# Attention output with d on partitions, in 64x32 array tiles and shared TensorE blocks, in a fused attention-and-MoE kernel

## The chip, the cores and the metric

One core of one Trainium2 chip. The metric is device microseconds (us) of one execution of the whole program. The kernel before takes 190.25 us, the median of three runs (190.19 to 191.84). TensorE is called PE below, VectorE DVE, ScalarE ACT, GpSimd POOL. A "pair" is one weight load and the matmul that uses it: two PE instructions.

## The reference

```python
# attention: q, k, v, alpha are (4, 8, 768, 48)
for t in range(S):
    state = alpha[:, :, t, :, None] * state + np.einsum('bhd,bhe->bhde', k[:, :, t], v[:, :, t])
    y[:, :, t] = np.einsum('bhd,bhde->bhe', q[:, :, t], state)
# MoE: x is y reordered to (3072, 384); w_in (384, 2048), w_out (2048, 384)
h = x @ w_in
r = np.maximum(h, 0.0)
return (r * r) @ w_out
```

The kernel computes the recurrence in chunks: inside a chunk by masked scores, between chunks through a state of 48 x 48 numbers per head. It works in 12 units, each of 256 time steps of one batch entry.

## The kernel before

A small list scheduler in the kernel orders all work. Each `add("pe", ...)` below is one block of PE instructions that is never split: the scheduler takes the block of highest priority whose inputs its own model says are there.

Of one unit's PE blocks these matter here (cut):

```python
def kv(pe):                                   # what a chunk adds to the state
    for p in range(NPR):
        for j in range(2):
            for ab in halves:
                ro = slice(ab * HP, (ab + 1) * HP)
                ins = pe.matmul(psY[ab][:, p * 96:p * 96 + 96],
                                QKS[qs][ro, 0, j, 2 * p:2 * p + 2, :].rearrange("p h d -> p (h d)"),
                                VBF[vb][ro, j, p * 96:p * 96 + 96], ...)
...
for hp in range(2):
    def score(pe, hp=hp, pb=pb):              # 16 matmuls in 64x64 tiles
        for i in range(2):
            p = 2 * hp + i
            for j in range(2):
                for ab in range(2):
                    for h in range(2):
                        ro = slice(64 * h, 64 * h + 64)
                        ins = pe.matmul(pb[ab * HP:(ab + 1) * HP, h, (2 * i + j) * C:(2 * i + j + 1) * C],
                                        KQT[kt][ro, 0, j, p, ab * HP:(ab + 1) * HP],
                                        KQT[kt][ro, 1, :, p, ab * HP:(ab + 1) * HP])
    add("pe", score, ...)                     # then the mask, on DVE
def y(pe):                                    # time on partitions
    ...  # 16 matmuls q x state, then 32 masked scores x v
add("pe", y, ...)
...  # two copies to XBF on ACT
def xt(pe):                                   # turns y so that d is on partitions, as the MoE wants it
    ...  # 6 transposing matmuls
add("pe", xt, ...)
...  # copy to XT on DVE
```

The MoE of a unit follows: s1 (48 matmuls of 256 columns) and s2 (32 of 384 columns), in blocks of 6 and 4. The block m1 computes running sums of log alpha.

```python
M1_FROM = 3
pa, pakey = (psTF[:], ("ps", "T")) if u >= M1_FROM else (psP[:, 0, :], ("ps", "P"))
```

## Time and profile before

| | before |
|---|---|
| time, us | 190.25 |
| span in the profile, us | 189.2 |
| PE matmuls | 2283 |
| PE busy | 94% |
| DVE / ACT / POOL busy | 59% / 69% / 46% |

From the page of the kernel before: busy time of the engines, the span in 40 slices of 4.7 us (a digit is a busy share in tenths), the queue that brings instructions, and the chain of work that ended last.

```profile
PE 178.7 (94%) x2283; PEld 125.4 (66%) x2283; DVE 112.3 (59%) x154; ACT 131.3 (69%) x253; POOL 86.8 (46%) x97
...
PE   7899899996989899999999999999999999999993
...
PEclk9999999999999999999999999999999999999999
DMA  6999999999999999981997982955315218110102
...
q8 instruction: 18, 0.29, 0.6%
...
PE 66%; DMA 15%; SPq 7%; DVE 5%; POOL 3%; issue 1%; ACT 1%; POOLq 0%; DVEq 0%
```

PE is the limit on paper: 94% busy. The DMA row: its engines are nearly full for the first 18 slices, about 85 us.

The wait view of PE (what it waited for, us in total, times, longest):

```profile
PE psY L628 <- DVE pm L615: 1.5, 1, 1.5
PE psO L387 <- DVE warm L378: 1.3, 1, 1.3
PE psH L687 <- ACT rr L696: 1.1, 2, 0.8
```

These and six smaller ones come to about 7 us. "Issue" is time in which PE waits for nothing that the profile shows.

The timeline of PE at one y (start, us, engine, line, operation, output <- inputs, weights, data, count). Durations overlap, so cost is read from start to start:

```profile
113.66 0.36 PE L628 MATMUL psY<-sbd,kqt 128*64 128x96 bf16 x8
113.86 0.34 PE L628 MATMUL psY<-sba,kqt 128*64 128x96 bf16 x8
114.12 0.57 PE L636 MATMUL psY<-vbf,pm 64*128 64x48 bf16 x32
114.63 1.48 PE L687 MATMUL psH<-xt,win 128*128 128x256 bf16 x12
```

L628 is the part of y that comes from the state, L636 that inside a chunk: y takes 0.97 us, from 113.66 to 114.63. The xt, elsewhere in the timeline, takes 0.34 and a kv 0.45.

### The profile page before, as it was taken

The numbers are of one execution on the slowest core, as the hardware profiler recorded it, in microseconds if no ns is written. First come the engines' busy times: TensorE is split into PE (matmuls) and PEld (weight loads), VectorE is DVE, ScalarE is ACT, GpSimd is POOL, SyncE is SP. The second block draws the span as 40 slices with busy tenths as digits, with TensorE's granted clock in tenths as the row PEclk, the third lists the DMA queues.
The fourth block names the chain that finished last, engine by engine and source line by source line (L and its number), as shares of the span: only waits on it lengthen the run. The fifth ranks groups of instructions, "written<-read, shape, count | busy, mean of one in ns | idle before, by whom it ended". The sixth has DMA issues, their size and how long they took to land.

```text
span 189.2 us, 5328 instructions
## 1 busy us (share of the span) xinstructions
PE 178.7 (94%) x2283; PEld 125.4 (66%) x2283; DVE 112.3 (59%) x154; ACT 131.3 (69%) x253; POOL 86.8 (46%) x97
## 2 busy tenths in 40 slices
PE   7899899996989899999999999999999999999993
PEld 2345676674566577768677767676677687677771
DVE  6788662889959449748368576267156185441230
ACT  2658799878696667858849749579567476477552
POOL 6224686635284356554735725534723354243100
PEclk9999999999999999999999999999999999999999
DMA  6999999999999999981997982955315218110102
GB/s 156 325 364 377 385 371 268 268 287 286 291 228 263 225 225 309 201 236 42 142 319 108 247 250 53 238 157 71 85 45 97 59 42 114 42 45 27 56 3 83
DMA packets 76119, 34.95 MB, mean 185 GB/s; under 512 B 69440, under 2 KB 74560, under 8 KB 76096
## 3 DMA queue, kind: packets, MB, share of 16 engines
q1 hardware_dynamic: 76096, 34.61, 71.4%
q8 instruction: 18, 0.29, 0.6%
q14 instruction: 5, 0.04, 0.1%
HBM read 25.17 MB, written 4.72 MB: 158 GB/s over the span
## 4 chain that ended last, share of the span: by engine, by line
PE 66%; DMA 15%; SPq 7%; DVE 5%; POOL 3%; issue 1%; ACT 1%; POOLq 0%; DVEq 0%
PE psH L687 28%; PE psO L717 25%; DMA raw<-in_q_dram 7%; SPq L470 6%; DMA stg<-in_moe_w_in_dram 5%; PE psP L608 4%; DMA kqt<-qks 3%; PE psY L636 2%; PE psY L628 2%; DVE pm L615 2%; DVE qks L531 2%; PE psY L573 2%; PE psTF L654 1%; PE psH L717 1%; POOL gt L703 1%
## 5 line engine op out<-in xcount | busy, mean ns | idle before, releaser
L703 POOL TENSOR_TENSOR gt<-rr 128x512 bf16<-128x512 bf16 x45 | 52.3, 1165 | 56.5 <-ACT rr L696 51.9
L687 PE MATMUL psH<-xt,win 128*128 128x256 bf16 x576 | 72.3, 273 | 1.1 <-ACT rr L696 1.1
L717 PE MATMUL psO<-wout,gt 128*128 128x384 bf16 x368 | 68.9, 326 | 1.6 <-ACT gt L700 1.1
L696 ACT ACTIVATE rr<-psH 128x512 bf16<-128x512 f32 x96 | 56.8, 598 | 10.7 <-PE psH L687 9.2
L687 PEld LDWEIGHTS psH<-xt,win 128*128 128x128 bf16 x576 | 53.9, 98 | 12.2 <-ACT rr L696 1.4
L717 PEld LDWEIGHTS psO<-wout,gt 128*128 128x128 bf16 x368 | 34.3, 98 | 21.0 <-ACT gt L700 1.2
L615 DVE TENSOR_TENSOR pm<-psP,mask 128x1024 bf16<-128x1024 f32 x23 | 28.1, 1223 | 18.9 <-PE psP L608 18.9
L703 DVE TENSOR_TENSOR gt<-rr 128x512 bf16<-128x512 bf16 x28 | 18.5, 662 | 28.2 <-ACT rr L696 28.2
L725 ACT ACTIVATE osb<-psO 128x384 f32<-128x384 f32 x23 | 11.3, 489 | 27.2 <-PE psO L717 27.0
L531 DVE TENSOR_TENSOR qks<-raw,asb 128x768 bf16<-128x768 f32 x24 | 29.2, 1250 | 1.3 <-ACT asb L519 1.3
L500 POOL TENSOR_TENSOR raw<-raw,ral 128x384 f32<-128x384 f32 x12 | 12.1, 1005 | 8.3 <-ACT ral L495 7.1
L492 ACT ACTIVATE lab<-raw 128x768 bf16<-128x768 f32 x12 | 10.1, 843 | 6.8 <-DVE raw L490 6.8
L700 ACT ACTIVATE gt<-rr 128x512 bf16<-128x512 bf16 x23 | 14.4, 627 | 0.4
L387 PE MATMUL psO<-warm 128*128 128x512 bf16 x43 | 13.4, 442 | 1.3 <-DVE warm L378 1.3
L648 ACT ACTIVATE xbf<-psY 128x384 bf16<-128x384 f32 x24 | 10.6, 493 | 3.7 <-PE psY L636 3.6
L660 DVE COPY xt<-psTF 128x768 bf16<-128x768 bf16 x12 | 6.7, 556 | 10.3 <-PE psTF L654 10.3
L593 POOL TENSOR_TENSOR sba<-tmp,acm 128x384 bf16<-128x384 f32 x8 | 6.6, 830 | 10.9 <-DVE tmp L591 10.9
L593 POOL TENSOR_TENSOR sbd<-tmp,acm 128x384 bf16<-128x384 f32 x8 | 7.3, 915 | 7.7 <-DVE tmp L591 7.7
L524 ACT ACTIVATE vbf<-rav 128x768 bf16<-128x768 f32 x12 | 10.1, 840 | 0.5 <-DMA rav<-in_v_dram 0.5
L490 DVE TENSOR_TENSOR raw<-raw 128x384 f32<-128x384 f32 x12 | 8.3, 688 | 3.1 <-DMA raw<-in_alpha_dram 3.1
L608 PE MATMUL psP<-kqt 64*64 64x128 bf16 x368 | 9.6, 222 | 0.4 <-ACT kqt L558 0.2
L608 PEld LDWEIGHTS psP<-kqt 64*64 64x64 bf16 x368 | 5.9, 106 | 5.7 <-issue 3.5
(68 smaller groups left out, 141.9 us busy)
## 6 DMA issues: line engine op xcount, KB each, us to landing
raw<-in_alpha_dram SPq DMA_DIRECT2D x12, 384.0 KB, 5.1
raw<-in_k_dram SPq DMA_DIRECT2D x12, 384.0 KB, 4.7
raw<-in_q_dram SPq DMA_DIRECT2D x12, 384.0 KB, 4.9
rav<-in_v_dram SPq DMA_DIRECT2D x12, 384.0 KB, 5.1
out_dram<-osb SPq DMA_DIRECT2D x24, 192.0 KB, 2.1
stg<-in_moe_w_in_dram SPq DMA_DIRECT2D x4, 768.0 KB, 8.0
stg<-in_moe_w_out_dram SPq DMA_DIRECT2D x4, 768.0 KB, 7.4
kqt<-qks SPq DMA_TRANSPOSE x18, 3.7
```

Source lines behind the costliest of these rows:

```text
L387: o = Op("pe", lambda pe: pe.matmul(psO[:, 0:512], WARM[:, 0:128], WARM[:], start=not begun, stop=True, skip_group_check=True), 216, 0, "w")
L470: chain("sp", lambda e, dst=dst, src=src: e.dma_start(dst, src), 400, 2 * u * P - 4 * P + o, writes=[key], name=f"ld{nm}{u}", dma=f"{nm}{v ...
L500: add("pool", lambda e: e.tensor_tensor(q0, q0, heads(RAL[0][:]), ALU.mult), 1000, pu + 520, reads=[("raw", r, 1), ("ral",)], writes=[("ra ...
L531: add("dve", lambda e, t=t: e.tensor_tensor(QKS[qs][:, t, :, :, 0:D].rearrange("p j h d -> p h j d"), RAW[r][:, t, :, :].rearrange("p h (j ...
L593: add("pool", lambda e, dst3=dst3, acm=acm, ab=ab: e.tensor_tensor(dst3, TMP[ab][:].rearrange("p (n d) -> p n d", d=D), acm, ALU.mult), 10 ...
L608: ins = pe.matmul(pb[ab * HP:(ab + 1) * HP, h, (2 * i + j) * C:(2 * i + j + 1) * C], KQT[kt][ro, 0, j, p, ab * HP:(ab + 1) * HP], KQT[kt][ ...
L615: add("dve", lambda e, pm=pm, pb=pb: e.tensor_tensor(PM[pm][:].rearrange("p h i s -> p (h i) s"), pb[:, :, :].rearrange("p h (i s) -> p (h ...
L687: ins = pe.matmul(psH[:, hb, i * n:(i + 1) * n], WIN[:, kk, fj * 128:(fj + 1) * 128], XT[:, kk, g0 * C:g0 * C + n], start=(kk == 0), stop= ...
L696: add("act", lambda e, hb=hb, rb=rb: e.activation(RR[rb][:], psH[:, hb, :], AF.Relu), act_ns(512), pu + 600, reads=[("ps", "H", hb)], writ ...
L700: add("act", lambda e, sq=sq, dst=dst: e.activation(dst, sq, AF.Square), 560, pu + 1200, reads=[("rr", rb)], writes=[("gt", gt, u)], name= ...
L703: add(how, lambda e, sq=sq, dst=dst: e.tensor_tensor(dst, sq, sq, ALU.mult), {"dve": 560, "pool": 1100}[how], pu + 1200, reads=[("rr", rb) ...
L717: ins = pe.matmul(po, GT[gt][:, fj, ti * C:(ti + 1) * C], WOUT[:, fj, :], start=(fj == 0), stop=(fj == FT - 1))
```

## The change

The intent: PE is the limit, so spend less of it per unit. y is computed with d on partitions, so xt and one of the two ACT copies go; DVE now copies half of y itself to XT (6.7 us in all, as its copy of xt took before). All attention matmuls use tiles of 64 rows x 32 columns, eight at once where before four 64x64 tiles ran. In y the program never lets the upper and the lower rows write the same PSUM bank at once: they change banks behind a semaphore (more on it under "What could not be tried"). From unit 5 on, kv and a score share one block and so do y and the next unit's score, which saves changes of tiling. States keep only their used columns. MOE_OFF moves the MoE later in the schedule.

The core of the diff (cuts marked with `...`):

```diff
+    def kv_part(u):
+        r, vr, la, a, qs, kt, vb = bufs(u)
+        halves = range(1 if is_last(u) else 2)
+
+        def fn(pe):
             for p in range(NPR):
                 for j in range(2):
-                    for ab in halves:
-                        ro = slice(ab * HP, (ab + 1) * HP)
-                        ins = pe.matmul(psY[ab][:, p * 96:p * 96 + 96],
-                                        QKS[qs][ro, 0, j, 2 * p:2 * p + 2, :].rearrange("p h d -> p (h d)"),
-                                        VBF[vb][ro, j, p * 96:p * 96 + 96], start=(p == 0 and j == 0),
-                                        stop=(j == 1), skip_group_check=True)
+                    for q4 in range(4):
+                        for ab in halves:
+                            ro = slice(ab * HP, (ab + 1) * HP)
+                            h, d0 = 2 * p + q4 // 2, 32 * (q4 % 2)
+                            ins = pe.matmul(psY[ab][32 * q4:32 * q4 + 32, p * D:(p + 1) * D],
+                                            QKS[qs][ro, 0, j, h, d0:d0 + 32], VBF[ro, vb, j, h, 16:DP],
+                                            start=(p == 0 and j == 0), stop=(j == 1), skip_group_check=True)
             return ins
...
+        return (fn, KV_NS, [("qks", qs, 0), ("vbf", vb)], [("ps", "Y", ab) for ab in halves], 2 * u * P + 2700,
+                f"kv{u}")
...
+    def score_part(u, hp):
+        kt = u % NKQT
+        pb, key = (psH, [("ps", "H", 0), ("ps", "H", 1)]) if u == 0 and hp else (psP, [("ps", "P")])
+
+        def fn(pe):
+            for i in range(2):
+                p = 2 * hp + i
+                for j in range(2):
+                    for q4 in range(4):
+                        ab = q4 // 2
+                        for h in range(2):
+                            ro = slice(64 * h, 64 * h + 64)
+                            ins = pe.matmul(pb[32 * q4:32 * q4 + 32, h, (2 * i + j) * C:(2 * i + j + 1) * C],
+                                            KQT[kt][ro, 0, j, p, 32 * q4:32 * q4 + 32],
+                                            KQT[kt][ro, 1, :, p, ab * HP:(ab + 1) * HP])
+            return ins
+
+        return fn, P_NS, [("kqt", kt, 0), ("kqt", kt, 1)], key, 2 * u * P + 3800 + 10 * hp, f"p{hp}{u}"
...
+        g0b, g1a = rounds(inter(0, 1)), [] if first else rounds(inter(1, 0))
+        g0a, g1b = ([] if first else rounds(inter(0, 0))) + rounds(intra(0)), rounds(inter(1, 1)) + rounds(intra(1))
+        if SWAP_SEM:
+            streams = (g0b + g0a, [[]] * len(g0b) + g1b) if first else (g0b + g0a, g1a + g1b)
+        elif first:
+            streams = (g0b + g0a, [[]] * 3 + g1b)
+        else:
+            streams = (g0b + [[]] * 2 + g0a, [[]] + g1a + g1b)
+
+        def fn(pe):
+            begun = set()
+            for k in range(max(len(s) for s in streams)):
+                if SWAP_SEM and k == len(g0b):
+                    turns[0] += 1
+                    ins.then_inc(turn, 1)
+                    pe.wait_ge(turn, turns[0])
+                both = [s[k] if k < len(s) else [] for s in streams]
+                for c in range(4):
+                    for part in both:
+                        if not part:
+                            continue
+                        t, ab, w, x = part[c]
+                        ins = pe.matmul(psY[ab][32 * c:32 * c + 32, (t // 4) * C:(t // 4 + 1) * C], w, x,
+                                        start=(ab, c) not in begun, stop=True, skip_group_check=True)
+                        begun.add((ab, c))
...
+    SWAP_SEM = True
...
+    def block(*parts):
+        def fn(pe):
+            for p in parts:
+                ins = p[0](pe)
...
-        p0 = 2 * m * P + 22000
+        p0 = 2 * m * P + MOE_OFF          # 30000
...
+    FUSE_FROM = 5
...
+        if w >= FUSE_FROM:
+            block(kv_part(w), score_part(w, 1))
...
+        if u < U and u >= FUSE_FROM:
+            block(y_part(w), score_part(u, 0))
+        else:
+            block(y_part(w))
+            if u < U:
+                block(score_part(u, 0))
```

The matmuls of a unit's kv go from 16 to 64, of a score from 16 to 32, of y and xt from 54 to 96 (the last and the first chunks have fewer).

## The prediction

> **What bounds it now.** TensorE. The page gives PE 94% of 189.2 us; the chain that ended last is 66% PE, from about 64 us unbroken PE work but for one evacuation at the end. The waits view gives PE only about 7 us of waits, nearly all before 64 us. Until about 80 us DMA is near its ceiling (slice row), yet PE has MoE work to fill in: it is busy with useful matmuls from 19 us on. The two MoE groups take, by the starts of instructions, 109 ns x 576 = 63 us and 162 ns x 384 = 62 us, and don't change. ACT 69%, DVE 59%, POOL 46% are not limits.
>
> So what counts is PE time per attention unit (12 units). From the starts of blocks in the timeline: m1 0.29, inter-chunk y 0.46, intra y 0.51, transpose xt 0.34, kv 0.45, two scores 0.35 each, and each change of array tiling costs: the MoE block before a tiled block is 1.42 instead of 1.31 us (0.11 in), and of the score's 350 ns only 4 x 56 are matmuls (0.126 out). In total about 3.1 us a unit.
>
> **What changes, costed.**
> - Scores become 32 instead of 16 matmuls each, in 64x32 tiles: eight tiles at once instead of four. In the trace four 64x64 tiles start within 10 ns, rounds 56 ns apart. I estimate the same 4 x 56 ns with eight tiles. [...] no trace here shows eight yet.
> - kv: 64 matmuls, 8 rounds of 48 columns. Estimate 26 to 35 ns a round, 0.21 to 0.28, plus 0.24 for the switches: saves 0.1.
> - y gives d on partitions, so xt (0.34), its DVE copy (6.7 us in all) and one of two ACT evacuations go. y is 12 rounds of 128 columns, 0.67, plus the semaphore between row groups: 216 ns of the last matmul, about 50 ns to the waiter as DVE's mask shows, a restart, less one round: about 0.24. So 1.14 with switches, against 1.37 with xt.
> - From unit 5 on kv+score and y+score share a block, each saving one switch, 0.24. [...]
> - m1 loses one 28 ns matmul.
> - State work on half the columns: DVE about 5 us, POOL about 6 us less in all; off the path.
>
> Sum: seven fused units save about 0.83 us each, five early ones 0.17 to 0.36 each (the first chunk had only half the inter-chunk work, but still needs 12 rounds). About 6.8 us, nearly all on the critical path, as PE has backlog throughout. I add nothing for DVE, ACT and POOL; MOE_OFF only moves MoE later, where it runs dense.
>
> **Prediction: 183.5 us, 8 in 10 between 180.5 and 187.5. Faster by over 2%: 0.80; within 2%: 0.16; slower: 0.04.**
>
> **What would show it right.** PE blocks: kv+score about 0.56 us from its first matmul to the next block, y+score about 1.26; rounds of eight 56 ns apart; one gap of about 0.29 us inside each y; no transposes to the xt; MoE groups still 109 and 162 ns apart; PE again without waits after 64 us; DVE near 107 us, ACT near 126.
>
> **What would make it wrong.** [...] kv rounds bound by weight loads at 56 ns: 2 to 3 us back. A semaphore gap of 0.5 us: 2.5 us back. Fused blocks waiting on the mask (1.2 us on DVE) or the transposing DMA. New PE idle in the DMA-bound first 70 us.

The sum came to about 6.8 us, and 190.25 less 6.8 is 183.5. The trace of before stands behind these estimates as far as it goes. Rounds of two matmuls of 48 columns start 25 ns apart (the inner y, 114.2 to 114.5 us), near the 26 of the kv; for the 35 the record names no source, nor for weight loads as a bound of the kv rounds. The score's last matmul is recorded as 216 ns long, the mask on DVE starts 51 ns after its end, and the first round of a score takes 80 ns and not 56 (the restart). The state work that is halved took 11.0 us on DVE and 13.9 on POOL.

## The result, and the profile after

The kernel after takes 202.06 us, the median of four runs (200.34 to 203.53; the run of 203.53 is not in the ratio). Executions over 1.5% slower than the fastest of the same kernel are left out of the means. The ratio to the kernel before is 1.056 (95%: 1.047 to 1.066): slower by 5.6%. A ratio here is the mean time of one kernel's fast runs over the mean of the other's in the same rounds, so it is not quite the ratio of the medians. The prediction, 183.5, had the wrong sign.

The same lines of the page of the kernel after (its slices are 5.0 us):

```profile
PE 179.5 (90%) x3609; PEld 123.5 (62%) x3613; DVE 104.1 (52%) x150; ACT 127.9 (64%) x241; POOL 83.3 (42%) x93
...
PE   7986598788997949977999999999999999999994
...
PEclk9999999999999996999999999999999999999999
DMA  6999999998999997999998105928143511010112
...
q8 instruction: 28, 0.46, 1.0%
...
PE 63%; DMA 13%; SPq 10%; ACT 5%; issue 5%; DVE 4%
```

PE is hardly busier in us, but it is idle more: the digits 5, 7, 4, 7, 7 all lie before slice 20. One digit of PEclk is a 6. The chain has 5% "issue". The instruction queue moves 28 packets.

The wait view of PE:

```profile
PE psY L578 <- issue: 3.0, 2, 2.7
PE psH L748 <- issue: 2.4, 2, 1.8
...
PE psP L617 <- issue: 1.3, 1, 1.3
```

The waits "for nothing" are new. The largest in the timeline:

```profile
70.70 0.60 PE L578 MATMUL psY<-vbf,qks 64*32 64x48 bf16 x56
73.97 0.22 PE L578 MATMUL psY<-vbf,qks 64*32 64x48 bf16 x8 [2.66 <-issue]
74.11 0.42 PE L617 MATMUL psP<-kqt 64*32 64x128 bf16 x32
74.46 0.87 PE L748 MATMUL psH<-xt,win 128*128 128x256 bf16 x6
75.12 2.77 PE L778 MATMUL psO<-wout,gt 128*128 128x384 bf16 x8
```

PE stops for 2.7 us after 56 of a kv's 64 matmuls. Nothing in the program stands between the 56th and the 57th: no wait, no change of tiling, no new buffer. The s2 matmuls of the last line then start 319 ns apart instead of 162: the clock record of the trace has PE at half clock from 75.1 to 78.5 us.

**Where the stops fall.** I numbered PE's own records (weight loads, matmuls and the few of its sequencer) together, in the order of their starts. There are six stops of over 0.25 us inside blocks, and all have a number that leaves 188 to 192 when divided by 256:

| stop begins, us | 16.4 | 21.1 | 46.8 | 71.1 | 93.8 | 105.8 |
|---|---|---|---|---|---|---|
| from last start to next start, us | 0.69 | 2.08 | 0.83 | 2.85 | 1.50 | 0.55 |
| inside | y | s1 | s1 | kv | score | kv |
| this page of 256 was used up in, us | 5.8 | 4.0 | 4.8 | 2.1 | 3.7 | 3.7 |

In sum 8.5 us (a stop is counted from the start of the last instruction to the start of the next, so a little more than the idle time in the views). The instruction queue brings 28 packets of 16,384 bytes for 7283 PE records, 260 to a packet; in before 18 for 4613, 256 to a packet. That PE's records stop every so often at the same place modulo 256 suggests one packet, or page, for 256 instructions. The kernel before has no such stop; there a page of PE lasts 7.1 to 12.2 us.

For the six stops, and in the last two rows for later boundaries with DMA less busy, the times of the packet that came in between (which packets belong to PE is inferred from the order):

| previous page entered, us | packet starts | packet ends | PE resumes | turnaround, us |
|---|---|---|---|---|
| 10.55 | 14.75 | 15.71 | 17.05 | 6.5 |
| 17.05 | 20.75 | 21.73 | 23.16 | 6.1 |
| 41.98 | 45.34 | 46.27 | 47.62 | 5.6 |
| 68.97 | 71.65 | 72.64 | 73.97 | 5.0 |
| 90.07 | 92.93 | 93.86 | 95.30 | 5.2 |
| 102.10 | 104.12 | 105.04 | 106.35 | 4.3 |
| 129.74 | 130.75 | 131.88 | 133.26, a stop of 0.2 | 3.5 |
| 143.36 | 144.11 | 145.04 | 146.67, no stop | under 3.3 |

In each of these rows the packet comes only after the page before its own is entered. In the six rows of the stops, where the DMA engines are full, it starts 2.0 to 4.2 us after that; in the last two rows, where the slice of the packet has a DMA digit of 2 and of 1, after 1.0 and 0.8 us. Then it takes about 1 us, and PE goes on 1.3 to 1.4 us later. I read this as a load of instructions that queues behind the data; the runs below test it. Rows chosen by their stops could mislead, so here are all page boundaries of the 18 traces of this document. Where packets of data kept the engines over 85% busy (233 boundaries), half of the instruction packets start about 2.0 us or more after the page is entered; where under 40% (144 boundaries), half start within 0.8 us. The spread is wide (in the first group from 2.0 us before to 5.0 us after), so full DMA makes a late packet likely and not certain. And in every stop of these traces PE goes on 1.1 to 1.6 us after a packet of the instruction queue has ended: it is the packet that ends the stop. A stop is what the turnaround takes beyond the time in which the page was used up: 0.7 us in the first row (6.5 less 5.8), 2.9 in the fourth (5.0 less 2.1). Over all of these traces a packet comes at most 2.3 us before the page before its own is entered (in before at most 1.3 us, at 149.1 us for a page entered at 150.4).

**What else moved.** Late in the run, with DMA light, blocks can be read undisturbed. A fused kv and score, and a fused y and score:

```profile
115.79 0.71 PE L578 MATMUL psY<-vbf,qks 64*32 64x48 bf16 x64
116.31 0.48 PE L617 MATMUL psP<-kqt 64*32 64x128 bf16 x32
116.73 0.61 PE L748 MATMUL psH<-xt,win 128*128 128x256 bf16 x4
...
128.84 0.71 PE L690 MATMUL psY<-kqt,sta 64*32 64x128 bf16 x32
129.37 0.74 PE L690 MATMUL psY<-pm,vbf 64*32 64x128 bf16 x64
129.90 0.48 PE L617 MATMUL psP<-kqt 64*32 64x128 bf16 x32
130.32 0.50 PE L748 MATMUL psH<-xt,win 128*128 128x256 bf16 x3
```

kv takes 0.53 us (116.31 less 115.79), the block 0.94. y and score take 1.48 (130.32 less 128.84). In the records of single instructions about the first 64 of such a block, 32 pairs, run at full pace (in y counted anew from its semaphore): from round to round 55 to 56 ns in y after the first, and 39, 27 and 26 in the kv of 93.24 us, whose next round comes after 128. From there on a pair starts every 8.3 ns, so a round of eight takes 67 ns and not 56. It is 8.3 ns for the 48 columns of a kv as for the 128 of a score, so the columns do not set it. I call it issue; what in PE sets it is not shown.

And the first units come late. After, at the second unit:

```profile
36.73 0.33 PE L498 MATMUL psP<-lab,lblk 128*128 128x384 bf16 x1
...
38.38 0.42 PE L617 MATMUL psP<-kqt 64*32 64x128 bf16 x32
...
40.71 0.29 PE L690 MATMUL psY<-kqt,sta 64*32 64x128 bf16 x8 [1.35 <-DVE pm L627]
```

The same score and y before:

```profile
25.36 0.42 PE L608 MATMUL psP<-kqt 64*64 64x128 bf16 x16
...
27.34 0.36 PE L628 MATMUL psY<-sba,kqt 128*64 128x96 bf16 x8
```

The y of unit 1 starts 13.4 us later. Ahead of its score now stands an m1 that writes the same psP: the m1 of unit 2, whose inputs arrive only then. Counting MoE matmuls at 109.3 and 162.5 ns each, before has done 56.3 us of MoE work by 100 us, after 45.9. The spans differ by 10.9 us; nearly all of it is there by 100 us. (Attention is behind as well, by about a unit: the y of unit 6 starts at 100.7 us in before, that of unit 5 at 101.3 in after. The gain late in the run makes up for that.)

### The profile page after: what moved, and what is told of

Its sections match the earlier page's. It is cut to its first block, busy times and chain, and to the rows that moved or that the text cites. A ratio compares the mean times of both kernels' runs of the same rounds, so it can differ in the third digit from the quotient of the medians.

```text
span 200.1 us, 7982 instructions
## 1 busy us (share of the span) xinstructions
PE 179.5 (90%) x3609; PEld 123.5 (62%) x3613; DVE 104.1 (52%) x150; ACT 127.9 (64%) x241; POOL 83.3 (42%) x93
## 4 chain that ended last, share of the span: by engine, by line
PE 63%; DMA 13%; SPq 10%; ACT 5%; issue 5%; DVE 4%
PE psH L748 25%; PE psO L778 25%; SPq L463 9%; PE psY L690 5%; DMA stg<-in_moe_w_in_dram 4%; PE psP L617 3%; DMA raw<-in_alpha_dram 3%; DMA rav<-in_v_dram 3%; DMA kqt<-qks 3%; PE psY L578 2%; DVE qks L521 2%; ACT rr L757 1%; PE psH L778 1%; ACT win L436 1%; DVE pm L627 1%
## 5 line engine op out<-in xcount | busy, mean ns | idle before, releaser
L748 PE MATMUL psH<-xt,win 128*128 128x256 bf16 x576 | 73.8, 273 | 3.1 <-issue 2.4
L764 POOL TENSOR_TENSOR gt<-rr 128x512 bf16<-128x512 bf16 x45 | 49.9, 1110 | 53.4 <-ACT rr L757 53.4
L521 DVE TENSOR_TENSOR qks<-raw,asb 128x768 bf16<-128x768 f32 x24 | 27.5, 1162 | 7.8 <-ACT asb L508 7.8
L601 POOL TENSOR_TENSOR sta<-tmp,acm 128x192 bf16<-128x192 f32 x16 | 13.0, 815 | 21.3 <-DVE tmp L599 21.2
L722 DVE CAST xt<-psY 128x384 bf16<-128x384 f32 x12 | 6.7, 557 | 17.7 <-PE psP L617 14.0
L617 PE MATMUL psP<-kqt 64*32 64x128 bf16 x736 | 11.1, 225 | 3.0 <-DMA kqt<-qks 1.3
L719 ACT ACTIVATE xt<-psY 128x384 bf16<-128x384 f32 x12 | 5.9, 490 | 10.3 <-PE psP L617 5.8
L617 PEld LDWEIGHTS psP<-kqt 64*32 64x32 bf16 x736 | 7.4, 91 | 5.8 <-issue 2.2
L578 PE MATMUL psY<-vbf,qks 64*32 64x48 bf16 x640 | 7.1, 186 | 4.2 <-issue 3.0
L690 PE MATMUL psY<-pm,vbf 64*32 64x128 bf16 x768 | 9.7, 221 | 0.8 <-issue 0.5
## 6 DMA issues: line engine op xcount, KB each, us to landing
stg<-in_moe_w_in_dram SPq DMA_DIRECT2D x4, 768.0 KB, 10.3
```

The source lines that it names most:

```text
L521: add("dve", lambda e, t=t: e.tensor_tensor(QKS[qs][:, t, :, :, 0:D].rearrange("p j h d -> p h j d"), RAW[r][:, t, :, :].rearrange("p h (j ...
L617: ins = pe.matmul(pb[32 * q4:32 * q4 + 32, h, (2 * i + j) * C:(2 * i + j + 1) * C], KQT[kt][ro, 0, j, p, 32 * q4:32 * q4 + 32], KQT[kt][ro ...
L690: ins = pe.matmul(psY[ab][32 * c:32 * c + 32, (t // 4) * C:(t // 4 + 1) * C], w, x, start=(ab, c) not in begun, stop=True, skip_group_chec ...
L748: ins = pe.matmul(psH[:, hb, i * n:(i + 1) * n], WIN[:, kk, fj * 128:(fj + 1) * 128], XT[:, kk, g0 * C:g0 * C + n], start=(kk == 0), stop= ...
L764: add(how, lambda e, sq=sq, dst=dst: e.tensor_tensor(dst, sq, sq, ALU.mult), {"dve": 560, "pool": 1100}[how], pu + 1200, reads=[("rr", rb) ...
```

## The experiments

Theories:

- **F, fetch.** Denser instructions use up a page sooner than the next can be fetched. PE stops.
- **I, issue rate.** Beyond the first 32 pairs of a block a pair costs 8.3 ns, so 32-column tiles give less than estimated.
- **Q, order.** New block order and fused blocks make the first units, and all MoE behind them, late: m1 of unit 2 ahead of the second score of unit 1; y of unit 4 in one block with a score of unit 5, for which it must wait.
- **M, MoE offset.** MOE_OFF alone delays MoE work that PE then lacks.

All results in one table. Stops are those of over 0.25 us at the same place modulo 256, inside a block, from each profile. "MoE" is the MoE work done by 100 us, as above. The ratio is to the kernel before, run on the same chip in the same session.

| run | what it is | us | ratio (95%) | stops: n, us | y of unit 1 / 4 starts | MoE |
|---|---|---|---|---|---|---|
| before | | 190.25 | 1 | 0 | 27.3 / 74.2 | 56.3 |
| after | | 202.06 | 1.056 (1.047 to 1.066) | 6, 8.5 | 40.7 / 89.1 | 45.9 |
| a_t64 | after, kv and scores in 64x64 | 194.60 | 1.013 (1.005 to 1.020) | 3, 4.4 | 38.7 / 82.7 | 49.8 |
| a_off22 | after, MOE_OFF of before | 200.42 | 1.043 (1.036 to 1.051) | 8, 8.7 | 40.1 / 80.8 | 50.9 |
| a_nofuse | after, no fused blocks | 199.92 | 1.047 (1.039 to 1.054) | 6, 8.0 | 40.7 / 78.9 | 47.0 |
| b_p32 | before, scores in 64x32 | 190.64 | 0.998 (0.991 to 1.006) | 0 | 27.6 / 74.1 | 56.5 |
| a_m2 | after, m1 from unit 2 on elsewhere | 199.32 | 1.046 (1.041 to 1.050) | 8, 9.1 | 29.6 / 86.3 | 49.6 |
| a_t64_m2 | both | 191.02 | 1.002 (0.999 to 1.005) | 2, 1.0 | 25.4 / 81.6 | 53.9 |
| a_thin | after, few late input bytes | 197.01 | 1.033 (1.025 to 1.041) | 3, 4.8 | 41.8 / 86.8 | 47.5 |
| b_thin | before, the same | 190.33 | 0.998 (0.994 to 1.002) | 0 | 27.3 / 73.5 | 56.8 |
| a_shift | after, 120 extra weight loads first | 209.27 | 1.095 (1.089 to 1.101) | 7, 11.8 | 44.8 / 92.0 | 43.3 |
| a_t64_m2_off22 | a_t64_m2, MOE_OFF of before | 194.43 | 1.020 (1.013 to 1.027) | 2, 2.0 | 25.6 / 82.3 | 51.9 |
| a_best | a_t64_m2, first score inside y | 190.95 | 1.000 (0.995 to 1.006) | 4, 4.6 | 25.5 / 81.1 | 52.2 |
| a_best22 | a_best, MOE_OFF of before | 195.11 | 1.024 (1.017 to 1.030) | 3, 2.6 | 25.2 / 81.1 | 53.5 |
| a_f7 | after, fused from unit 7 | 206.23 | 1.073 (1.066 to 1.080) | 8, 13.8 | 41.7 / 81.2 | 44.7 |
| a_t64_m2_f7 | a_t64_m2, fused from unit 7 | 190.99 | 0.994 (0.988 to 0.999) | 1, 0.8 | 25.4 / 75.8 | 55.7 |
| a_best_f7 | a_best, fused from unit 7 | 193.05 | 0.995 (0.986 to 1.004) | 3, 3.1 | 26.2 / 78.9 | 52.4 |
| a_best_f8 | a_best, fused from unit 8 | 187.95 | 0.979 (0.973 to 0.985) | 1, 1.0 | 25.5 / 75.7 | 54.2 |

All gave the reference's result but a_thin and b_thin, which are wrong. Stops, starts and MoE come from one profiled run each. The medians are of all runs, slow ones too (one each in after, a_t64 and a_off22, two in a_best_f7); the ratios are of fast runs alone. Runs come from four sessions besides that of after, and before took 190.5 to 191.7 us in them (medians). So a difference of us between sessions is good to about 1 us, and the ratios are the fairer measure. By them after loses 10.7 us to before, a_t64 is 8.3 us under after, a_off22 2.5, a_m2 2.1, a_nofuse 1.9, a_t64_m2 10.3, a_thin 4.5; a_f7 is 3.1 and a_shift 7.4 over it.

### a_t64: fewer, larger tiles for kv and scores

```diff
-                    for q4 in range(4):
+                    for q2 in range(2):
...                      # kv: 64-row and 64-column tiles, 32 matmuls for 64
-                    for q4 in range(4):
-                        ab = q4 // 2
+                    for ab in range(2):
...                      # score: 16 matmuls for 32
```

> The kernel after, with kv and score back in 64x64 tiles (same rows, same columns, half the matmuls); y stays in 64x32. Theory F (fetch): PE stops at fixed places, every 256 PE instructions, because pages of instructions are used up faster than the next one lands; 8 such stops cost about 8.5 us in the trace of after. Fewer instructions in a burst (about 5,750 PE records instead of 7,283) should leave 3 us of stops or less. Theory I (issue): beyond the first 64 instructions of a block one weight load and matmul pair takes 8.3 ns, so 64-matmul kv blocks take 0.6 us; here kv falls to 0.25 to 0.35 us and scores to 4 x 56 ns, about 3 us in all. F and I together: 191 to 194 us. Theory O (order: later MoE and fused blocks hold PE up): stays at 200 to 202 us.

Measured 194.60 us, 7.5 us under the kernel after, with 5879 PE records for 7283 and three stops of 4.4 us in all. The time lies just above the range I gave, 191 to 194, and the stops, 4.4 us, are more than the 3 I expected. The fall of 4.1 us in stops (8.5 less 4.4) is a good half of the gain; the rest I put down to the kv, bound by issue, and to the clock that no longer fell (mean granted clock of the profiled runs 1.000 for 0.991), without having parted them. In blocks late in the run: a full kv and a score take 0.60 us where after has 0.94, but y and a score take 1.56 where after has 1.48, as the tiling now changes inside that block. F and I both get support; this run does not part them.

### b_p32: the opposite, one denser block in the kernel before

```diff
-                        for ab in range(2):
+                        for q4 in range(4):
+                            ab = q4 // 2
...                          # score: 32 matmuls for 16, as in after
```

> The kernel before with only the scores in 64x32 tiles: 368+ more matmuls, as many more weight loads, in 24 separate blocks with MoE work around them. F (it is the rate in a burst, not the count): no stop at a 256 boundary, as a page still lasts 6 us or more. I: each block lasts 32 x 8.3 = 267 ns instead of 224, in all +1 us: 190.8 to 192. If instead every further page of instructions costs a stop of 1 us or so whatever the rate: 193.5 or more.

Measured 0.998: the same. The cost of I that I expected here did not come: the scores take 9.76 us in sum (from start to next start) against 9.71, so 32 pairs in a block that stands alone run at full pace. Only the two scores of unit 0, which follow each other without a break, take longer: from their first start to their last 538 ns with 64 pairs, 425 ns before with 32. It shows that eight tiles at once are no problem by themselves, and no stops appear when only the scores get denser. What a longer block pays beyond its first 32 pairs, 8.3 ns for each pair, is read from the traces; its cause is not shown.

### a_off22: the MoE at its old offset

```diff
-    MOE_OFF = 30000
+    MOE_OFF = 22000
```

> The kernel after with MOE_OFF at the 22000 of before. O: the time falls by 4 us or more, to 198 or less, since MoE work again fills PE in the first 100 us. F: stops at 256-instruction boundaries stay at 6 us or more and the time stays within 2 us of 202.

Measured 200.42, 1.6 us under after. More MoE work is done by 100 us (50.9), but there are two more stops. I had said that M would take off 4 us or more; M is no main cause.

### a_nofuse: no shared blocks

```diff
-    FUSE_FROM = 5
+    FUSE_FROM = 99
```

> The kernel after with no block fused (FUSE_FROM 99). F: the stops after 90 us (about 2.2 us) shrink because MoE matmuls stand between the bursts, while 14 switches of about 0.24 us return (3.4 us): 201 to 204 us. O, if fused blocks waiting for their slowest input are the trouble: 3 us or more faster, 199 or less.

Measured 199.92, 2.1 us under after. The y of unit 4 starts at 78.9 and not 89.1, so that wait of Q is real. Stops stay at 8.0 us (the largest is 3.31), and none comes after 81.9 us. Fused blocks are not needed for the stops. The time lies in neither of the two ranges I gave, 199 or less and 201 to 204.

### a_m2: the early m1 in its own buffer

```diff
-    M1_FROM = 3
+    M1_FROM = 2
```

> The kernel after with M1_FROM 2 instead of 3: m1 of unit 2 no longer shares the PSUM banks psP with the second score of unit 1. Theory Q (block order): after emits m1 of unit 2 ahead of that score, so it waits for unit 2's inputs (landed at about 36 us), y of unit 1 starts at 40.7 us instead of 27.3 in before, and PE has nothing to do but warm-up matmuls around 30 us. Q: y of unit 1 starts at 27 to 30 us, MoE work done by 40 us rises from 10.4 to about 13.5 us, the time falls by 2 to 4 us to 198 to 200; the stops at 256 boundaries stay. If Q is not on the path: within 1 us of 202.

Measured 199.32, 2.7 us under after. The y of unit 1 starts at 29.6 and not 40.7: one shared buffer made that order. But stops rose to 9.1 us: the work that came earlier ran into pages.

### a_t64_m2: both

> Both repairs: kv and score in 64x64 tiles, and M1_FROM 2. If the two act apart, as theories F with I and Q say: 194.6 less 2 to 4 us, 190.5 to 192.5, near before. If the early PE gaps would come anyway (inputs still land late): 194 or more.

The edit is that of a_t64 and of a_m2 together. Measured 191.02, the time of the kernel before (ratio 1.002), with two stops of 1.0 us in all. The medians fall by 7.5 us with a_t64, by 2.7 with a_m2, by 11.0 with both (by the ratios 8.3, 2.1 and 10.3). So the loss of 11.8 us is found but for about one, and the times add up within the noise. The stops do not (8.5 us fall to 4.4 with one, rise to 9.1 with the other, and are 1.0 with both): one edit moves the place of the pages for the other.

What stays is the fused wait. In the timeline of a_t64_m2:

```profile
76.57 0.82 PE L777 MATMUL psO<-wout,gt 128*128 128x384 bf16 x4 [0.78 <-DVE gt L763]
...
78.89 2.77 PE L777 MATMUL psO<-wout,gt 128*128 128x384 bf16 x16 [0.58 <-ACT osb L785]
81.59 0.71 PE L689 MATMUL psY<-kqt,sta 64*32 64x128 bf16 x32
...
82.80 0.42 PE L616 MATMUL psP<-kqt 64*64 64x128 bf16 x16
```

The masks that y (L689) needs were done at 75.3 us. But its block ends with the score (L616) of unit 5, and the transfers that turn that unit's k and q were issued at 74.5 and 76.5 and landed at 78.6 and 80.6. So y could not start before 80.6, and PE waited for MoE inputs in between.

### a_thin and b_thin: the same instructions, few bytes

```diff
+            if u >= NRAW:
+                src, dst = src[0:8], dst[0:8]
```

The inputs of units 3 to 11 are loaded for 8 of 128 partitions only: wrong values, the same program otherwise. A kernel whose stops come from full DMA must gain; the kernel before must not.

> Wrong result on purpose: the kernel after, but from unit 3 on each input load moves 8 of 128 partitions, so that DMA is nearly idle after 40 us while PE's instructions stay the same. F: from a page's first instruction to the first of the next page that had to be waited for took 4.2 to 6.1 us under DMA load and 3.5 us in the light-load end of the trace; so with thin loads the stops after 40 us shrink from about 5.8 us (without unit 1's and 2's) to 1.5 us or less. If the stops have another cause (PE queue, PSUM, tile mode), they stay at 4 us or more.

> Wrong result on purpose: before with the same thin loads, as the partner of a_thin. No stops in either case. If fetch stops under DMA load and inputs that come late are what turns the change into a loss, a_thin is within 3 us of b_thin (after lost 11.6 us with full loads). If the longer time comes from PE's work itself, a_thin is still 8 us or more behind.

Measured: b_thin 190.33, no change; a_thin 197.01, 5.1 us under after (medians; two runs each). I expected the two within 3 us of each other; they are 6.7 apart, so that was missed. The trace says why: a_thin's first two stops, at 16.4 and 19.7 us (3.2 us in sum), and the late y of unit 1 come before its thin loads do. After 40 us it has one stop of 1.6 us (I had said 1.5 or less in sum) where after has 5.7 us. It is the largest stop of after, at the same record, again behind a page that was used up in 2.1 us: with DMA nearly idle the turnaround is 3.7 us instead of 5.0, and the stop 1.59 us instead of 2.85. The stop, and the DMA row of a_thin's page (slices of 4.9 us):

```profile
69.54 0.60 PE L580 MATMUL psY<-vbf,qks 64*32 64x48 bf16 x56
71.54 0.22 PE L580 MATMUL psY<-vbf,qks 64*32 64x48 bf16 x8 [1.40 <-issue]
...
DMA  6999999710644013916331107146055410020112
```

So the lighter DMA load takes away most of the later stops (1.6 us for 5.7), as F says, and the gain of b_thin, none, shows that lighter input alone does nothing for a kernel without stops.

### a_shift: the same program, 120 instructions later

```diff
+            for _ in range(shift):            # 120, before the first matmul only
+                pe.ldweights(WARM[:, 0:128])
```

If stops belong to places in the code, they stay with their code. If they belong to pages of 256 instructions, they move to other code and keep the same number modulo 256.

> The kernel after with 120 more weight loads of the warm-up operand before PE's first matmul, where PE has nothing to do. All later PE instructions stand 120 places further on. F: stops inside blocks stay at the same place modulo 256 of PE's own count, so they hit other code (not the second half of kv of unit 4 or the middle of s1 of unit 0), their sum may change by some us either way (2 to 12 us), and the time with it, 198 to 206. If the stops belong to the code (tile mode, PSUM bank, a data wait), they stay at the same matmuls and move to another place modulo 256.

Measured 209.27, above what I had expected. There are seven stops, 11.8 us in sum, all at the number 194 modulo 256 (after: 188 to 192), and in other code. Stops that belonged to their code would have moved by 120, to about 55. The first of them, in the timeline of a_shift (its L626 is the score, L587 kv):

```profile
17.18 0.36 PE L626 MATMUL psH<-kqt 64*32 64x128 bf16 x17
20.14 0.41 PE L626 MATMUL psH<-kqt 64*32 64x128 bf16 x15 [2.60 <-issue]
...
59.35 0.59 PE L587 MATMUL psY<-vbf,qks 64*32 64x48 bf16 x54
61.57 0.23 PE L587 MATMUL psY<-vbf,qks 64*32 64x48 bf16 x10 [1.63 <-issue]
```

A score that ran through in after is cut after 17 of its 32 matmuls. Moving the program by 120 instructions moved the stops: they belong to pages. Of the 7.2 us by which a_shift is slower than after, 3.3 are stops (11.8 less 8.5). The trace also has three spells of half clock of 3.4 us each, where after has one (one of them, from 108.6 us, follows a stop of 2.30 us, from 105.3 to 107.6); two more can cost 3.4 us at most. And m1 of unit 0 starts 4.2 us later, because of the 120 loads ahead of it. How much of these two reaches the end isn't separated.

### a_t64_m2_off22, a_best, a_best22: offset again, and a score inside y

a_best fills the gap at y's semaphore. The first score of the next unit, in 64x32 tiles as y has, goes between the two parts of y, and is no longer paced behind 96 pairs:

```diff
                     ins.then_inc(turn, 1)
+                    if between is not None:
+                        between(pe)
                     pe.wait_ge(turn, turns[0])
```

> The kernel with both repairs (191.0 us), and MOE_OFF 22000 besides. The same one-number change took after from 202.1 to 200.4. O: 1 to 2 us faster again, 189 to 190. If its gain in after came from a lucky place of the page boundaries: within 0.7 us of 191.0.

> Both repairs, the first score of fused blocks in 64x32 again, and put between the two row-group parts of y, so that its 32 matmuls (about 0.27 us) run in the gap of 0.32 us that the semaphore between row groups leaves. If that gap is PE time lost: 7 fused units x (0.25 us of gap + 0.2 us of a switch between 64x32 and 64x64 spared) = 3 us: 188 to 189.5. If the gap or the switch are hidden behind something else: 190.5 or more. 224 more matmuls and loads may bring a stop back (1 us).

> The kernel a_best with MOE_OFF 22000. O: 1 us or more under a_best. Otherwise within 1 us of it.

Measured 194.43, 190.95 and 195.11. With MOE_OFF at 22000 both kernels lose about 4 us (3.4 and 4.2), where after itself gained 1.6. I had expected no such loss. Stops do not explain it (a_best22 has fewer than a_best), and why the offset changes its sign stays open. a_best did what it should in a unit: from the y of unit 6 to that of unit 11, five units, PE's time beyond the MoE's is 3.11 us a unit in before, 2.62 in after, 2.57 in a_t64, 2.56 in a_t64_m2 and 2.39 in a_best (0.14 of it a stop). Yet its time is that of a_t64_m2, and not the 188 to 189.5 I had given: stops went from 1.0 to 4.6 us, with 227 more PE records (6086 less 5859).

### a_f7, a_t64_m2_f7, a_best_f7, a_best_f8: fuse later

```diff
-    FUSE_FROM = 5
+    FUSE_FROM = 7      # or 8
```

> The kernel after with fused blocks from unit 7 on instead of 5. If a fused block that waits for the next unit's transposes costs time: y of unit 4 at about 80 instead of 89.1 us, and 1 to 3 us faster, 199 to 201. It cannot say more, since the stops move too.

> Both repairs, fused from unit 7 on. Two units lose the saved switches (2 x 2 x 0.24 = 1 us). If the fused block's wait held PE up: y of unit 4 at 75 to 77 us instead of 81.6, MoE work done by 100 us up from 53.9 by 1 to 3 us, time 188 to 190. If not: 191 to 192.

> The kernel a_best, fused from unit 7 on. If the fused wait counts: 187 to 189.5, the first version under before; stops of 1 to 4 us decide where in that range. If not: 190.5 to 192.

> The kernel a_best, fused from unit 8 on: one more unit without the saved switches (+0.5 us against a_best_f7), unless unit 7's transposes come late as well; then up to 1 us faster than a_best_f7. Place of the page boundaries adds about 2 us either way.

Measured 206.23, 190.99, 193.05 and 187.95. In a_f7 the y of unit 4 starts at 81.2 instead of 89.1, as wanted, but the kernel is 4.2 us slower than after, where I had expected 1 to 3 us faster: stops are 13.8 us. One of them, of 1.7 us at 173.5, comes with DMA nearly idle (digits 0 and 1 in its slices): a fused y and score used up a page in 2.3 us, and the turnaround was 4.0 us (171.3 to 175.2). So a page that is used up fast enough stops PE without load on DMA, as in a_thin; with the load stops were more and longer (after against a_thin: 5.7 us in sum after 40 us against 1.6, and 2.85 us against 1.59 at the same record).

In a_t64_m2_f7 the y of unit 4 starts at 75.8 and the kernel is at 0.994 of before, a small gain, less than the 188 to 190 us I had given. a_best_f7 is inconclusive: it ran from 190.3 to 195.2 us, two of its four runs slow, the profiled one among them. a_best_f8 is the fastest: 0.979, 2.1% under the kernel before, and clearly faster; that it is so by more than 2% is not certain, as the interval (0.973 to 0.985) straddles 0.98. Its page:

```profile
PE 173.5 (94%) x2964; PEld 119.6 (64%) x2964; DVE 108.3 (58%) x150; ACT 127.5 (69%) x241; POOL 82.1 (44%) x93
...
PE   7898899998977889999999999999999999999993
```

And one of its y with the score inside:

```profile
154.51 0.30 PE L694 MATMUL psY<-kqt,sta 64*32 64x128 bf16 x16
154.64 0.49 PE L619 MATMUL psP<-kqt 64*32 64x128 bf16 x32
154.93 0.35 PE L694 MATMUL psY<-kqt,sta 64*32 64x128 bf16 x16
155.06 0.75 PE L694 MATMUL psY<-pm,vbf 64*32 64x128 bf16 x64
155.74 0.99 PE L784 MATMUL psO<-wout,gt 128*128 128x384 bf16 x5
```

y and score take 1.23 us (155.74 less 154.51), where the kernel after has 1.48 (130.32 less 128.84). One stop of 1.0 us is left, at 18.1. PE is 94% busy again in a shorter span. How much of the difference between a_best_f7 and a_best_f8 is the fused wait and how much is the luck of the pages isn't settled; their stops differ by 2.1 us, but those of a_best_f7 are read in a slow run.

### What could not be tried

Without the semaphore between the row groups, nothing in this order of matmuls keeps two row groups from writing the same part of a PSUM bank at once; I took that for a race and did not run it, so no run here shows what it does. The kernel also holds an order without semaphore (SWAP_SEM = False, with the two groups shifted against each other); it was not run either. So the semaphore's whole price was not measured by leaving it out. Its gap is: 319 ns from the last start before it to the first after it.

## Why the prediction was wrong

**The step that failed: "About 6.8 us, nearly all on the critical path, as PE has backlog throughout."** The saving per unit was there, in smaller size (0.49 us for 0.83, below). But in the first 90 us there was not always work that PE could do: it lives on inputs, masks and transfers that arrive one by one, and now also on pages of instructions. In place of the backlog the runs showed PE stopped for instructions (six times, 8.5 us) and the y of units 1 and 4 late (2.7 and 2.1 us, each by its own undoing). 10.4 us of MoE work was missing at 100 us, out of 10.9 us in the span.

**What the list of risks left out: the load of instructions.** The change took PE's records from 4613 to 7283 and put them into bursts. A page of 256 that had lasted at least 7.1 us now lasted down to 2.1 us, with a turnaround of 4.3 to 6.5 us under full DMA. Six stops cost 8.5 us, and behind the longest seven s2 matmuls ran 319 instead of 162 ns apart, at half clock: 1.1 us more. Shown by the records, by a_shift (stops move with the count) and, for the part of the DMA load in the stops after 40 us, by a_thin. The line of 18 packets in the page of before (for 4566 weight loads and matmuls, 254 to a packet), and the count of matmuls in the diff, were there to be read: 3609 less 2283 matmuls, two instructions each, at 254 to a packet, gives ten more; 28 less 18 is ten.

**"New PE idle in the DMA-bound first 70 us" was on the list, without a size.** It came as theory Q in two places. The shared psP put the m1 of unit 2 ahead of the second score of unit 1 (13.4 us later y; a_m2: 2.7 us of the time). The fused block made y of unit 4 wait for unit 5 (y 10.2 us later than in a_nofuse; time 2.1 us). That too was on the list, as "Fused blocks waiting on the mask (1.2 us on DVE) or the transposing DMA", and without a size.

**"kv: ... 26 to 35 ns a round, 0.21 to 0.28".** It took 0.53 us, twice that and more than all of the old kv (0.45 with its switch). I had costed the array, not the issue: after the first 32 pairs a pair starts every 8.3 ns, and a round of eight takes 67 ns. The score in a fused block has the same term: its rounds are 67 ns and not 56.

**"I estimate the same 4 x 56 ns with eight tiles."** Right for a score that stands alone (b_p32: 9.76 against 9.71 us for all scores). The eight tiles of a round start 3 to 4 ns apart (in the y at 128.84 us).

**The semaphore "about 0.24"** from a gap of 0.29: the gap measured 0.32. Close. **Leaving a tiled block** was estimated at 0.126; in after it takes about 0.15 us (157 ns from the last start to the next block's first, less a pair). **Other engines**: DVE 104.1 us (predicted near 107), ACT 127.9 (near 126): right, and they were not limits.

**The saving per fused unit, "about 0.83 us each".** Measured from the y of unit 6 to that of unit 11, it was 0.49 in after (3.11 less 2.62). About all of the missing 0.34 is in the two fused blocks that the prediction had named. y and score take 1.48 us for the predicted 1.26: 0.22 a unit. kv and score take 0.94 with a full kv and 0.64 with a half one (the last chunk of a batch entry needs only half), for 0.56: 0.14 a unit on the average of these five, one full and four half. Two runs give it back: kv and score take 0.60 in a_t64, y and score 1.23 in a_best. Fusing itself saved 0.33 us a unit (2.95 in a_nofuse less 2.62), where the prediction had two switches of 0.24.

**"MOE_OFF only moves MoE later, where it runs dense"** is not settled: undoing it helped after by 1.6 us and hurt a_t64_m2 by 3.4.

A rough count of the 11.8 us: 8.5 of stops, 1.1 of half clock, 2.7 and 2.1 of the two waits (each by its own undoing), less about 3.4 us of gain late in the run (7 units at 0.49). The sum is 11.0. The parts overlap, as a_f7 and a_best show, so its closeness proves little; each part has its own run or record, the half clock the record alone.

## What to carry to other kernels

Splitting matmuls into more, smaller tiles paid here in instructions for what it bought in array time: before doing it, count the PE instructions in each stretch and set the time in which 256 of them run against the turnaround of a packet of the instruction queue: here 4.3 to 6.5 us at the stops with DMA full, and 3.7 (a_thin) and 4.0 (a_f7) at stops with DMA nearly idle. Two blocks that are joined wait for the inputs of both, and a shared buffer fixes their order; join only where inputs have long been there. Here joining from unit 8 on gave the fastest version, though its lead over unit 7 is not explained. When an edit changes instruction counts, stops move to other places, so compare counts of stops as well as times before calling one edit better than another.
